# Channel-mix matrices loaded as f64 words and converted behind the attention stage, without a DRAM scratch; the copy of k by the scalar engine

## The chip, the cores and the metric

One NeuronCore of a Trainium2 chip runs the whole kernel. Its engines are TensorE (PE; its weight loads are listed apart as PEld), VectorE (DVE), ScalarE (ACT), GpSimd (POOL) and SyncE (SP), which here only issues DMAs. Each engine works through its own queue in order; a matmul, a copy or a DMA issue that waits for data holds up all that stands behind it in that queue. The metric is the time of one execution on the device, in microseconds (us).

## The reference

Three layers follow each other, on 4 batches of 768 tokens with 384 channels:

```
# 1. linear attention with decay, 8 heads of 48
y[t] = r[t] @ (state + (u*k[t]) v[t]^T);  state = w[t]*state + k[t] v[t]^T
# 2. four attention experts of 64 dims, causal softmax, the best two of four per token, weighted
q, k, v = x@wq[e], x@wk[e], x@wv[e];  out += mask*gate * (softmax(q k^T/8) @ v @ wo[e])
# 3. channel mix (all three matrices come as float64)
xk, xr = mu_k*x + (1-mu_k)*x_prev,  mu_r*x + (1-mu_r)*x_prev
out = sigmoid(xr @ w_r) * (max(xk @ w_k, 0)**2 @ w_v)      # 384x384, 384x1024, 1024x384
```

## The kernel before

The three layers are written as three streams: **A** (layer 1, two heads at a time: 16 pairs), **B** (layer 2, `phase_b`, one batch at a time) and **C** (layer 3; `c_thin` in units of 256 tokens for batches 0 to 2, `c_wide` in units of 384 tokens for batch 3). Products that must be exact are made of a high and a low part of each factor (`split`), three matmuls for one.

Stage 1 runs A for all batches, with about the first one and three quarters batches of B beside it. When A is done, its SBUF (pool `pA`) is given up, and stage 2 runs the rest of B beside C; then C's wide units end the kernel. `run_all` hands out pieces of the streams by their costs, and a list scheduler then fixes the order of instructions on each engine. Stage 2 lets C go first by a lead of a tenth of its cost (`CLAG`).

[...] `c_convert` turns them into two fp32r parts in 34 blocks of 256 or 192 columns during stage 1. Each block (`split_block`) is a load on SP's queue (L797), a scale on ACT (L802), three integer operations on DVE (L803 to L805), the high part on ACT (L807), the low part on POOL (L808), and two stores to a DRAM scratch on SP's queue (L817). At the start of stage 2, `c_weights` reads the scratch back with six loads from POOL's queue (L833). The names are `c_raw` for the words, `c_w` for the value, `c_hi` and `c_lo` for the parts, and ckh, ckl, crh, crl, cvh, cvl for the parts of the three matrices.

In C, `c_mix` makes the two mixed inputs (`mh`, `ml` by L858 to L865), `c_hidden` the product with w_k (`ph`, eight groups of nine matmuls, L871), its square on POOL (`rl`, L891) and its parts (`hh`, `hl`), and `c_out` the products with w_r (`pz`) and w_v (`pvo`).

In B, `proj` makes q and k of two experts. The high part of k must also stand on the other 64 partitions, and a DMA on SP's queue copies it there (L571, 32 of them). `trans` copies transposed probabilities (`at`) from PSUM, some on DVE (L692), the rest on ACT (L694): the tables `AT_DVE` (batches below `AT_B`) and `AT_DVE2` say which.

Of the kernel before, what the change touches and what calls it, by code (L numbers as in the profile page):

```python
# [112 lines left out]
def rwkv_moe_kernel(ctx, tc, r, k, v, w, u, wg, wq, wk, wv, wo, mu_k, mu_r, w_k, w_v, w_r, out):  # L113
# [666 lines left out]
    CW = (("ck", w_k, KT, FF), ("cr", w_r, KT, DM), ("cv", w_v, NF, DM))  # L780
    csc = {
        nm: [nc.dram_tensor(f"{nm}_{x}_scratch", (128, n0 * n1), F32R, kind="Internal").ap() for x in "hl"]
        for nm, _, n0, n1 in CW
    }

    CQ_L, CQ_S = nc.sync, nc.sync

    def split_block(src, hi, lo, n):
        T = lambda tag, dt: pA.tile([128, n], dt, tag=tag, name=tag, bufs=CB, padded_shape=[128, 256])
        if src.dtype != I64:  # L790
            st = T("c_w1", F32)
            nc.sync.dma_start(st, src)
            nc.scalar.copy(hi, st)
            nc.gpsimd.tensor_tensor(out=lo, in0=st, in1=hi.bitcast(F32), op=OP.subtract)
            return
        raw = pA.tile([128, 2 * n], U32, tag="c_raw", name="c_raw", bufs=CB, padded_shape=[128, 512])
        CQ_L.dma_start(raw, src.bitcast(U32))  # L797
        wd = raw.rearrange("p (n two) -> p two n", two=2)
        wlo, whi = wd[:, 0], wd[:, 1]
        w1 = T("c_w1", U32)  # L800
# [1 line left out]
        nc.scalar.activation(out=w1.bitcast(F32), in_=whi.bitcast(F32), func=AF.Copy, scale=2.0 ** -112)  # L802
        V.tensor_scalar(out=w1, in0=w1, scalar1=3, scalar2=None, op0=OP.logical_shift_left)  # L803
        V.scalar_tensor_tensor(out=w1, in0=whi, scalar=0x80000000, in1=w1, op0=OP.bitwise_and, op1=OP.bitwise_or)
        V.scalar_tensor_tensor(out=w1, in0=wlo, scalar=29, in1=w1, op0=OP.logical_shift_right, op1=OP.bitwise_or)  # L805
        w1f = w1.bitcast(F32)
        nc.scalar.copy(hi, w1f)  # L807
        (V if CONV_DVE else nc.gpsimd).tensor_tensor(out=lo, in0=w1f, in1=hi.bitcast(F32), op=OP.subtract)  # L808

    def c_convert():  # L810
        pend = []
        for nm, src, n0, n1 in CW:
            n = 256 if n1 % 256 == 0 else n1 // 2
            for j in range(n0):
                for o in range(0, n1, n):
                    for d, t in pend:
                        CQ_S.dma_start(d, t)  # L817
                    hi = pA.tile([128, n], F32R, tag="c_hi", name="c_hi", bufs=CB, padded_shape=[128, 256])
                    lo = pA.tile([128, n], F32R, tag="c_lo", name="c_lo", bufs=CB, padded_shape=[128, 256])
                    split_block(src[j * 128 : (j + 1) * 128, o : o + n], hi, lo, n)  # L820
                    at = j * n1 + o
                    pend = [(csc[nm][i][:, at : at + n].bitcast(F32), t.bitcast(F32)) for i, t in enumerate((hi, lo))]
                    yield 1
        for d, t in pend:
            CQ_S.dma_start(d, t)
# [399 lines left out]
```

## Time and profile before

| | us |
|---|---|
| three timed runs, median (lowest to highest) | 726.49 (726.14 to 726.61) |
| profiled execution | 727.12 |
| its span in the trace | 725.4 |
| PE, PEld busy | 672.8, 585.4 |
| DVE, ACT, POOL busy | 497.9, 409.2, 299.7 |

The span is what the trace covers; the 1.7 us that the profiled execution has beyond it lie around it. The shares of busy time are averages over stages that differ, so the tables below cut the span into stretches. Stage 1 reaches to about 326 us, where the six loads of the weights are issued; the matmuls of layer 3 begin at 333 us, and B ends at about 645 us. The granted clock of TensorE was 0.984 of full speed over the span.

### The profile page before, as it was taken

Reading aid. Unit: us, or ns where it says so; the run is one execution under the profiler, and the core shown is the slowest. Engines: PE = TensorE matmul, PEld = TensorE weight load, DVE = VectorE, ACT = ScalarE, POOL = GpSimd, SP = SyncE. Lnnn points to the kernel's source line nnn. Section 1 sums busy time; section 2 is a strip of 40 time slices with the busy share of each in tenths; the row PEclk is TensorE's granted clock in tenths of the full one; section 3 lists DMA queues with packets and bytes.
Section 4 is the critical chain, followed back from the end, with each engine's and each line's share of the span. In section 5 each row is a group of like instructions: output and inputs, shape, how many; then the busy total and the mean of one; then the engine's idle time right before and its main releaser. Section 6 shows DMA issues by size and latency. Waiting matters only on the chain.

```text
span 725.4 us, 13681 instructions
## 1 busy us (share of the span) xinstructions
PE 672.8 (93%) x4938; PEld 585.4 (81%) x4938; DVE 497.9 (69%) x938; ACT 409.2 (56%) x1117; POOL 299.7 (41%) x397
## 2 busy tenths in 40 slices
PE   5887978889799999997999999999999999999995
PEld 4776856676577786866999899889898888989995
DVE  8988899998999888754543756556457573729520
ACT  3554556666576566656735657465556656534530
POOL 5876444343445222204625435362343515352320
PEclk9999899999999999999999999999999999999999
DMA  8797666668677653159320103211101101220001
GB/s 157 152 184 173 176 180 175 170 174 251 148 198 186 170 126 83 33 187 411 100 67 11 45 12 99 98 34 44 55 34 44 23 13 34 86 68 23 12 23 38
DMA packets 144205, 77.88 MB, mean 107 GB/s; under 512 B 109824, under 2 KB 138752, under 8 KB 143616
## 3 DMA queue, kind: packets, MB, share of 16 engines
q1 hardware_dynamic: 139936, 64.73, 35.1%
q0 software_dynamic: 864, 7.47, 2.6%
q10 hardware_dynamic: 3328, 4.72, 1.8%
q8 instruction: 41, 0.67, 0.4%
q14 instruction: 36, 0.29, 0.1%
HBM read 47.40 MB, written 23.99 MB: 98 GB/s over the span
## 4 chain that ended last, share of the span: by engine, by line
PE 64%; DVE 18%; DMA 8%; issue 4%; ACT 3%; POOL 1%; SPq 1%; ACTq 0%; DVEq 0%; POOLq 0%
PE ph L871 14%; PE pvo L871 14%; PE pz L871 5%; PE pa L710 5%; PE pq L518 4%; PE pt L681 3%; PE po L518 3%; PE py L368 3%; PE pv L518 3%; DMA c_raw<-in_moe_w_v_dram 2%; DVE ex L246 2%; PE psc L624 2%; PE pg L329 2%; DVE suf L220 2%; DVE rt L255 2%
## 5 line engine op out<-in xcount | busy, mean ns | idle before, releaser
L633 DVE TENSOR_REDUCE st<-psc 128x1 f32<-128x384 f32 (+4 forms) x128 | 62.1, 499 | 56.4 <-PE psc L629 41.3
L891 POOL TENSOR_TENSOR rl<-rl 128x256 f32<-128x256 f32 (+1 forms) x88 | 59.3, 678 | 78.5 <-ACT rl L890 78.3
L865 POOL TENSOR_TENSOR ml<-m,mh 128x256 fp32r<-128x256 f32 x54 | 40.6, 751 | 108.5 <-ACT mh L864 97.4
L645 ACT ACTIVATE A<-psc,st 128x384 f32<-128x384 f32 (+4 forms) x128 | 68.8, 542 | 20.2 <-DVE st L642 13.3
L871 PE MATMUL ph<-mh,ckh 128*128 128x256 f32 (+1 forms) x264 | 78.8, 299 | 0.9 <-ACT m L858 0.8
L871 PE MATMUL ph<-mh,ckl 128*128 128x256 f32 (+1 forms) x264 | 76.9, 292 | 1.5 <-DMA ckl<-ck_l_scratch 1.5
L338 POOL TENSOR_SCALAR_AFFINE_SELECT at<-at 128x512 f32<-128x512 f32 x48 | 44.7, 932 | 79.2 <-ACT at L337 79.0
L871 PE MATMUL ph<-ml,ckh 128*128 128x256 f32 (+1 forms) x264 | 76.9, 294 | 0.0
L871 PE MATMUL pvo<-cvh,hh 128*128 128x384 f32 x192 | 65.5, 341 | 0.0
L329 PE MATMUL pg<-rt,kt 128*128 128x256 f32 x192 | 53.8, 407 | 12.3 <-DVE um L307 5.8
L894 POOL TENSOR_TENSOR hl<-rl,hh 128x256 fp32r<-128x256 f32 x72 | 53.8, 756 | 27.0 <-ACT hh L892 26.7
L871 PE MATMUL pvo<-cvl,hh 128*128 128x384 f32 x192 | 64.6, 336 | 0.0
L871 PE MATMUL pvo<-cvh,hl 128*128 128x384 f32 x192 | 64.0, 336 | 0.0
L681 PE MATMUL pt<-ident,A 128*128 128x128 f32 x336 | 57.7, 275 | 0.0
L624 PE MATMUL psc<-k,q 128*128 128x384 f32 (+4 forms) x128 | 49.0, 383 | 9.0 <-ACT A L645 6.2
L890 ACT ACTIVATE rl<-ph 128x256 f32<-128x256 f32 (+1 forms) x88 | 35.5, 405 | 37.6 <-PE ph L871 26.2
L871 PEld LDWEIGHTS ph<-mh,ckh 128*128 128x128 f32 x264 | 49.9, 189 | 3.3 <-ACT m L858 1.0
L710 PE MATMUL pa<-at,vs 128*64 128x384 f32 (+2 forms) x288 | 52.1, 425 | 0.5 <-ACT at L694 0.5
L871 PEld LDWEIGHTS ph<-mh,ckl 128*128 128x128 f32 x264 | 50.0, 190 | 1.8 <-DMA ckl<-ck_l_scratch 1.8
L871 PEld LDWEIGHTS ph<-ml,ckh 128*128 128x128 f32 x264 | 49.9, 190 | 1.5 <-issue 1.5
L329 PEld LDWEIGHTS pg<-rt,kt 128*128 128x128 f32 x192 | 34.4, 197 | 19.8 <-DVE um L307 6.8
L861 DVE SCALAR_TENSOR_TENSOR m<-x2c,mu,m 128x256 f32<-128x256 f32 (+1 forms) x66 | 35.2, 539 | 20.4 <-ACT m L858 15.8
(172 smaller groups left out, 1917.3 us busy)
## 6 DMA issues: line engine op xcount, KB each, us to landing
x_scratch<-xs SPq DMA_DIRECT2D x24, 288.0 KB, 4.0
x<-x_scratch SPq DMA_DIRECT2D x6, 1152.0 KB, 8.4
nw<-in_w_dram SPq DMA_DIRECT2D x32, 144.0 KB, 3.7
nk<-in_k_dram SPq DMA_DIRECT2D x32, 144.0 KB, 3.1
nr<-in_r_dram SPq DMA_DIRECT2D x32, 144.0 KB, 2.8
nv<-in_v_dram SPq DMA_DIRECT2D x16, 288.0 KB, 3.2
out_dram<-rg SPq DMA_DIRECT2D x24, 192.0 KB, 1.9
c_raw<-in_moe_w_k_dram SPq DMA_DIRECT2D x12, 256.0 KB, 3.3
```

The lines of the kernel that those rows point to most:

```text
L329: nc.tensor.matmul(pg[:, x * 2 * C : (x + 1) * 2 * C], lhsT=kt[:, c * C : (c + 1) * C], rhs=rt[:, c].rearrange("p h x -> p (h x)"), start= ...
L338: nc.gpsimd.affine_select(out=av, in_=av, pattern=[[0, 4], [1, C]], compare_op=OP.is_gt, fill=0.0, base=0, channel_multiplier=-1)
L518: nc.tensor.matmul(out, lhsT=a, rhs=c, start=i == 0, stop=i == n - 1)
L624: nc.tensor.matmul(o, lhsT=qs[e][:, tsl], rhs=ks[e][:, s0:s1], start=True, stop=False, skip_group_check=True)
L633: nc.vector.tensor_reduce(out=st[:, si : si + 1], in_=o, axis=AX.X, op=OP.max, negate=True)
L645: nc.scalar.activation(out=A[:, s0:s1], in_=p[:, 0 : s1 - s0], func=AF.Exp, bias=nm, accum_out=st[:, 3 + si : 4 + si])
L681: nc.tensor.transpose(pt[:, (j - j0) * 128 : (j - j0 + 1) * 128], A[:, j * 128 : (j + 1) * 128], ident)
L710: nc.tensor.matmul(pa[64 * e : 64 * e + 64, t0:HALF], lhsT=vs[:, j, 2 * pr + e], rhs=at[e][:, c0 : c0 + HALF - t0], start=j == 0, stop=j = ...
L865: eng.tensor_tensor(out=lo[:, j], in0=m1, in1=hi[:, j].bitcast(F32), op=OP.subtract)
L871: nc.tensor.matmul(out, lhsT=a, rhs=c, start=i == 0, stop=i == n - 1)
L891: nc.gpsimd.tensor_tensor(out=rl_, in0=rl_, in1=rl_, op=OP.mult)
L894: eng.tensor_tensor(out=hl[:, m], in0=rl_, in1=hh[:, m].bitcast(F32), op=OP.subtract)
```

## The change

The constants: the table of `at` copies on DVE is empty for batch 0, and batch 1 now takes the longer table that held for batches 2 and 3. The copy of k to the other partitions is made by ACT from PSUM in batches 1 to 3; batch 0 keeps the DMA.

The conversion and the scratch are gone from stage 1. Stage 2 begins with 17 loads of 64-bit words (512 or 384 elements in each of 128 partitions) on POOL's queue, into the room that the parts of the same piece will take; ahead of them the first input tile of C now also goes through POOL's queue. The conversion of a piece is the same seven steps without the two stores: the value is built in a tile that borrows the room of the second mixed input (`mh1`, `ml1`), and the parts overwrite the words. Three pieces are converted before the first product with w_k, the others between its eight groups (1, 1, 1, 2, 2, 2, 5), and the second mixed input of the first unit comes after them all.

```diff
-DUP = "dma"
-AT_DVE = ((5, 0), (4, 0))
+AT_DVE = ()
 AT_DVE2 = ((5, 0), (4, 0), (3, 0))
-AT_B = 2
+AT_B = 1
...
                         split(ks[e][own, sl], kls[e][own, sl], src)
-                        if DUP == "act":
+                        if b:
                             nc.scalar.copy(ks[e][oth, sl], src)
...
                         else:
                             nc.sync.dma_start(ks[e][oth, sl].bitcast(F32), ks[e][own, sl].bitcast(F32))
...
+    CW = tuple(
+        [("ck", w_k, j, 512 * g, (4, 2, 128)) for g in range(2) for j in range(KT)]
+        + [("cr", w_r, j, 0, (1, 2, DM)) for j in range(KT)]
+        + [("cv", w_v, j, 0, (1, 2, DM)) for j in range(NF)]
+    )
+    def c_weight_loads(pW):
+        raws = []
+        for nm, src, j, o, (m, x, n) in CW:
+            words = 2 if src.dtype == I64 else 1
+            t = pW.tile([128, words * m * n], U32, tag=f"{nm}{j}_{o}", name="cw", bufs=1, padded_shape=[128, 2 * m * n])
+            nc.gpsimd.dma_start(t, src[j * 128 : (j + 1) * 128, o : o + m * n].bitcast(U32))
+            raws.append(t)
+        return raws
+    def c_convert(pW, raws, pool, tags=("mh1", "ml1")):
...
+                nc.scalar.activation(out=w1f, in_=whi.bitcast(F32), func=AF.Copy, scale=2.0 ** -112)
+                V.tensor_scalar(out=w1, in0=w1, scalar1=3, scalar2=None, op0=OP.logical_shift_left)
+                V.scalar_tensor_tensor(out=w1, in0=whi, scalar=0x80000000, in1=w1, op0=OP.bitwise_and, op1=OP.bitwise_or)
+                V.scalar_tensor_tensor(out=w1, in0=wlo, scalar=29, in1=w1, op0=OP.logical_shift_right, op1=OP.bitwise_or)
+            t = pW.tile([128, m, x, n], F32R, tag=f"{nm}{j}_{o}", name="cp", bufs=1)
+            v = w1f.rearrange("p (m n) -> p m n", n=n)
+            nc.scalar.copy(t[:, :, 0], v)
+            nc.gpsimd.tensor_tensor(out=t[:, :, 1], in0=v, in1=t[:, :, 0].bitcast(F32), op=OP.subtract)
+            wsp[nm, j, o] = t
+            yield 0
...
+        mixes[0] = [c_load(pool, *units[0], n, 1, nc.gpsimd), {}]
+        conv = c_convert(pW, c_weight_loads(pW), pool)
+        for _ in mix(0, 0):
+            pass
+        for _ in next_n(conv, KT):
+            yield 0
...
+            if u == 0:
+                side = (list(next_n(conv, i)) for i in (1, 1, 1, 2, 2, 2, 5))
+                side = (c for g in (side, mix(u, 1)) for c in g)
+                yield from c_side(c_hidden(pool, pst, mixes[u][1][0], n, 1, hs), side, 1)
...
-    conv = stream(c_convert(), nconv * CV)
-    run_all(sB, sA, conv, until=sA)
-    for _ in conv[0]:
-        pass
+    run_all(sB, sA, until=sA)
...
-        c_weights(pW)
```

The order of instructions, row by row as each engine's queue has them (line of the kernel, operation, output and inputs, size of the output, repeats). DVE in stage 1, where batch 0 of B begins, before: `rt`, `xs`, `kt`, `suf` and `ex` belong to A, `c_w` to the conversion.

```order
L246 SCALAR_TENSOR_TENSOR ex<-wx,d1f 128x774
L255 TENSOR_TENSOR rt_86<-ptr,ex 48x3x128 x4
L383 TENSOR_TENSOR xs<-py,xs 128x384
L803 TENSOR_SCALAR c_w_842<-c_w_842 128x256
L804 SCALAR_TENSOR_TENSOR c_w_842<-c_raw,c_w_842 128x256
L383 TENSOR_TENSOR xs<-py,xs 128x384
L805 SCALAR_TENSOR_TENSOR c_w_842<-c_raw,c_w_842 128x256
L256 TENSOR_TENSOR ku<-ku,nr 128x576
L220 SCALAR_TENSOR_TENSOR suf<-wx,d_77 128x775
```

The same place in the changed kernel (its line numbers are lower by two here):

```order
L244 SCALAR_TENSOR_TENSOR ex<-wx,d1f 128x774
L253 TENSOR_TENSOR rt_86<-ptr,ex 48x3x128 x4
L381 TENSOR_TENSOR xs<-py,xs 128x384
L254 TENSOR_TENSOR ku<-ku,nr 128x576
L381 TENSOR_TENSOR xs<-py,xs 128x384
L257 TENSOR_REDUCE cc<-ku 128x12
L218 SCALAR_TENSOR_TENSOR suf<-wx,d_77 128x775
```

The three `c_w` rows are gone, here and 33 times more down to the end of stage 1.

POOL at the start of stage 2, before: six loads, then the low part of the mixed input.

```order
L338 AFFINE_SELECT at<-at 128x512 x5
L833 DMA ckh<-ck_h_scratch 128x3072
L833 DMA ckl<-ck_l_scratch 128x3072
L833 DMA crh<-cr_h_scratch 128x1152
L833 DMA crl<-cr_l_scratch 128x1152
L833 DMA cvh<-cv_h_scratch 128x3072
L833 DMA cvl<-cv_l_scratch 128x3072
L844 MEMSET x2c 128x3
L616 MEMSET st_4601 128x6
L865 TENSOR_TENSOR ml_3893<-m_3894,mh_3892 128x256
```

The same place after (`cw` are the words of a piece, `cvs` the value, `cp` its parts):

```order
L336 AFFINE_SELECT at<-at 128x512 x5
L826 MEMSET x2c 128x3
L827 DMA x2c<-x_scratch 128x3x256
L790 DMA cw<-in_moe_w_k_dram 128x1024 x6
L790 DMA cw<-in_moe_w_r_dram 128x768 x3
L790 DMA cw<-in_moe_w_v_dram 128x768 x8
L847 TENSOR_TENSOR ml_3473<-m_3474,mh_3472 128x256
L612 MEMSET st_4302 128x6
L815 TENSOR_TENSOR cp<-cvs,cp 128x4x128 x2
L847 TENSOR_TENSOR ml_3473<-m_3479,mh_3472 128x256
```

Eighteen DMA issues stand where six stood, and the low parts of the weights are made between those of the mixed input.

PE just ahead of the first product with w_r (`pz`), before:

```order
L518 MATMUL pq<-x,wkl 128x384
L518 MATMUL pq<-x,wkh 128x384
L723 MATMUL pb<-ident,y 128x128
L710 MATMUL pa<-at_5025,vs 64x384
L710 MATMUL pa<-at_4726,vs 64x384
L710 MATMUL pa<-at_5025,vs 64x384
L710 MATMUL pa<-at_4726,vs 64x384
L871 MATMUL pz<-crh,mh_3941 128x384
```

The same place after; `psc`, `pt` and `pa` are now of the next batch of B:

```order
L620 MATMUL psc<-k_4621,q_4619 128x384
L621 MATMUL psc<-kl_121,q_4619 128x384
L677 MATMUL pt<-ident,A 128x128 x2
L706 MATMUL pa<-at_5206,vs 64x384
L706 MATMUL pa<-at_5162,vs 64x256
L706 MATMUL pa<-at_5206,vs 64x256
L706 MATMUL pa<-at_5162,vs 64x128
L706 MATMUL pa<-at_5206,vs 64x128
L853 MATMUL pz<-cp,mh_3732 128x384 x2
```

From the first `ph` to the first `pz` there were 167 matmuls in PE's queue before, 72 of them `ph`; now there are 303, again 72 of them `ph`. The 136 more are B's.

## Rows read from the trace of the kernel before

**Rows 1.** The stretches: PE, PEld, DVE, ACT, POOL busy (instructions), clock, DMA share, GB/s.
```profile
20.00:80.00 60.00, 51.79 (x466) 40.95 (x462) 52.75 (x76) 30.77 (x76) 46.17 (x42) 0.91 0.77 169
80.00:250.00 170.00, 148.67 (x1235) 118.42 (x1231) 156.36 (x316) 108.36 (x301) 70.33 (x79) 0.98 0.70 182
250.00:326.00 76.00, 72.14 (x627) 58.23 (x625) 57.12 (x124) 45.42 (x127) 15.91 (x21) 1.00 0.44 113
326.00:376.00 50.00, 46.26 (x298) 40.65 (x299) 27.65 (x49) 31.11 (x84) 23.14 (x37) 1.00 0.54 198
376.00:641.00 265.00, 265.00 (x1803) 241.09 (x1802) 149.66 (x290) 155.66 (x450) 111.09 (x166) 1.00 0.15 46
```
**Rows 2.** The chain that ended last, shares of the span by engine.
```profile
PE 64%; DVE 18%; DMA 8%; issue 4%; ACT 3%; POOL 1%; SPq 1%; ACTq 0%; DVEq 0%; POOLq 0%
```
**Rows 3.** The conversion on DVE, 80 to 250 us: line, operation, count | busy us, mean ns.
```profile
L805 DVE SCALAR_TENSOR_TENSOR c_w<-c_raw,c_w 128x192 uint32<-128x192 uint32 x22 | 11.6, 536 | 0.2
L804 DVE SCALAR_TENSOR_TENSOR c_w<-c_raw,c_w 128x192 uint32<-128x192 uint32 x22 | 7.7, 362 | 0.2
L803 DVE TENSOR_SCALAR c_w<-c_w 128x192 uint32<-128x192 uint32 x22 | 6.5, 302 | 1.0 <-ACT c_w L802 0.9
L805 DVE SCALAR_TENSOR_TENSOR c_w<-c_raw,c_w 128x256 uint32<-128x256 uint32 x10 | 5.5, 550 | 0.2
L804 DVE SCALAR_TENSOR_TENSOR c_w<-c_raw,c_w 128x256 uint32<-128x256 uint32 x10 | 4.3, 434 | 0.1
L803 DVE TENSOR_SCALAR c_w<-c_w 128x256 uint32<-128x256 uint32 x10 | 3.2, 324 | 1.1 <-ACT c_w L802 1.1
```
**Rows 4.** The conversion and the `at` copies elsewhere, whole span and 80 to 250 us.
```profile
L808 POOL TENSOR_TENSOR c_lo<-c_w,c_hi 128x192 fp32r<-128x192 f32 (+1 forms) x34 | 28.1, 830 | 47.7 <-ACT c_hi L807 27.4 <-issue 10.7 <-DMA cr_l_scratch<-c_lo 3.0
L802 ACT ACTIVATE c_w<-c_raw 128x192 f32<-128x192 f32 (+1 forms) x34 | 13.7, 402 | 12.0 <-DMA c_raw<-in_moe_w_v_dram 6.9 <-DMA c_raw<-in_moe_w_k_dram 2.6 <-DMA c_raw<-in_moe_w_r_dram 1.9
L807 ACT CAST c_hi<-c_w 128x192 fp32r<-128x192 f32 (+1 forms) x34 | 12.5, 374 | 13.2 <-DVE c_w L805 13.1
...
L692 DVE COPY at<-pt 128x512 f32<-128x512 f32 x8 | 5.5, 683 | 0.1
```
**Rows 5.** One line of the conversion: duration ns min/median/max, first and last start.
```profile
L805 DVE SCALAR_TENSOR_TENSOR c_w<-c_raw,c_w x34: 335/410/1252, 68.0 to 246.6; 128x192 uint32<-128x192 uint32 x22, 128x256 uint32<-128x256 uint32 x12
```
**Rows 6.** Copy of k: the ACT operation on its source, and PE's waits for the DMA.
```profile
L142 ACT CAST k<-pq x32: 453/474/478, 96.0 to 577.4; 64x384 fp32r<-64x384 f32 x32
...
PE psc L624 <- DMA k<-k: 2.2, 2, 1.7
```
**Rows 7.** POOL's queue from 324 us: start, duration, operation [idle before, releaser].
```profile
325.50 0.73 POOL L833 DMA_DIRECT2D ckh<-ck_h_scratch  x1 [14.92 <-PE pt L681]
326.22 0.55 POOL L833 DMA_DIRECT2D ckl<-ck_l_scratch  x1
...
328.30 0.59 POOL L833 DMA_DIRECT2D cvl<-cv_l_scratch  x1
...
331.42 0.73 POOL L865 TENSOR_TENSOR ml<-m,mh 128x256 fp32r<-128x256 f32 x1 [2.38 <-ACT mh L864]
```
**Rows 8.** PE at the first product of layer 3.
```profile
332.84 0.48 PE L871 MATMUL ph<-mh,ckh 128*128 128x256 f32 x2 [0.84 <-ACT m L858]
...
336.50 0.38 PE L871 MATMUL ph<-mh,ckl 128*128 128x256 f32 x1 [1.48 <-DMA ckl<-ck_l_scratch]
```
**Rows 9.** The chain of waits in order of time: start, us, what.
```profile
167.79 9.46 DMA c_raw<-in_moe_w_v_dram
...
326.22 10.23 DMA ckl<-ck_l_scratch
...
359.65 1.78 PE pz L871 x9
```
**Rows 10.** DMA issues: KB each, us from issue to landing.
```profile
cvl<-cv_l_scratch POOLq DMA_DIRECT2D x1, 1536.0 KB, 19.8
```

More of the change, by code (lines that the diff above doesn't have):

```diff
@@ L778, in rwkv_moe_kernel @@
     NF = FF // 128
[L780 to L800, printed above, removed]
-        V = nc.vector
[L802 to L825, printed above, removed]
-        yield 1
@@ new lines, in c_weight_loads @@
+    def c_weight_loads(pW):
[7 more added lines that the diff above has]
+    def c_convert(pW, raws, pool, tags=("mh1", "ml1")):
+        room = [
+            pool.tile([128, KT, TN], F32R, tag=t, name="cvs", bufs=1).rearrange("p k n -> p (k n)").bitcast(U32) for t in tags
+        ]
+        V = nc.vector
+        for i, ((nm, src, j, o, (m, x, n)), raw) in enumerate(zip(CW, raws)):
+            w1 = room[i % 2][:, 0 : m * n]
+            w1f = w1.bitcast(F32)
+            if src.dtype != I64:
+                nc.scalar.copy(w1f, raw.bitcast(F32))
+            else:
+                wd = raw.rearrange("p (n two) -> p two n", two=2)
+                wlo, whi = wd[:, 0], wd[:, 1]
+                nc.scalar.activation(out=w1f, in_=whi.bitcast(F32), func=AF.Copy, scale=2.0 ** -112)
[8 more added lines that the diff above has]
+            yield 0
@@ L875, in c_hidden @@
     def c_hidden(pool, pst, mix, n, bufs, res):
-        ckh, ckl = wsp["ck"]
+        ck = lambda j, m, x: wsp["ck", j, 512 * (m // 4)][:, m % 4, x]
         kh, kl = mix
@@ L885, in c_hidden @@
                 ph[:, 0:n],
-                [t for j in range(KT) for t in ((ckh[:, j, ms], kh[:, j]), (ckl[:, j, ms], kh[:, j]), (ckh[:, j, ms], kl[:, j]))],
+                [t for j in range(KT) for t in ((ck(j, m, 0), kh[:, j]), (ck(j, m, 1), kh[:, j]), (ck(j, m, 0), kl[:, j]))],
             ):
@@ L906, in c_out @@
                 pz[:, 0:DM],
-                [t for j in range(KT) for t in ((rh[:, j, cs], crh[:, j]), (rh[:, j, cs], crl[:, j]), (rl[:, j, cs], crh[:, j]))],
+                [t for j in range(KT) for t in ((rh[:, j, cs], cr(j, 0)), (rh[:, j, cs], cr(j, 1)), (rl[:, j, cs], cr(j, 0)))],
             ):
@@ L918, in c_out @@
             pv = pst("o", "pvo")
-            terms = [t for m in range(NF) for t in ((hh[:, m, cs], cvh[:, m]), (hh[:, m, cs], cvl[:, m]), (hl[:, m, cs], cvh[:, m]))]
+            terms = [t for m in range(NF) for t in ((hh[:, m, cs], cv(m, 0)), (hh[:, m, cs], cv(m, 1)), (hl[:, m, cs], cv(m, 0)))]
             for k in mm_seq(pv[:, 0:DM], terms, 8):
@@ L934, in rwkv_moe_kernel, with c_thin @@
     bdone = {"n": 0}
-    def c_thin(pool, pst, units, n):
+    def c_thin(pW, pool, pst, units, n):
         mixes, hs = {}, []
@@ L1076, in rwkv_moe_kernel @@
         thin_units = units_of(range(B - 1), TN)
-        thin = c_thin(pC, psum_of(psC, {x: ("c", 2) for x in "hzo"}), thin_units, TN)
+        thin = c_thin(pW, pC, psum_of(psC, {x: ("c", 2) for x in "hzo"}), thin_units, TN)
         left = B - sB[2]
@@ L1188, in rwkv_moe_kernel @@
         with ExitStack() as sg:
-            c_weights(sg.enter_context(tc.tile_pool(name="pW2", bufs=1, side="right")))
+            pW = sg.enter_context(tc.tile_pool(name="pW2", bufs=1, side="right"))
             pD = sg.enter_context(tc.tile_pool(name="pD2", bufs=1, side="left"))
+            for _ in c_convert(pW, c_weight_loads(pW), pD, ("cvs0", "cvs1")):
+                pass
             psD = sg.enter_context(tc.tile_pool(name="psD2", bufs=1, space=PSUM))
```

29 lines of the change are left out of this document (8 added, 21 removed).

## The prediction

> **What bounds the kernel now.** I read the stretches first [rows 1], then the chain of waits [rows 2, 9], then the groups by line for what the change takes out [rows 3, 4], and last the queues of POOL and PE where stage 2 begins [rows 7, 8].
>
> The stretches show two kernels. Up to 326 us DVE is the fullest engine: it is busy 156.36 of the 170 us from 80 to 250, or 92%, with ACT at 64%, POOL at 41% and PE at 87%. From 376 to 641 us PE is busy in all of the 265 us, its weight loads in 241.09, and DVE falls to 56% [rows 1]. The chain says the same: PE has 64% of it and DVE 18% [rows 2]; with PE leading in stage 2, DVE's part must come mostly from stage 1. So work taken off DVE is worth something before 326 us, and work given to DVE after 376 us is nearly free; what remains is the seam between them, where the change puts all of it at once.
>
> How tight is PE in stage 1? Its busy time leaves 170 - 148.67 = 21.3 us of idle from 80 to 250, which would cap any gain there. But the weight loads fill only 118.42 of 170 us, 70%, against 241.09 of 265, 91%, in the stretch where PE is certainly the bound [rows 1]. The Trainium skill (Perfetto Trace Analysis, Identifying the Most-Contended Engine) says that matmul busy time is no measure of PE's headroom, since pipelined matmuls overlap, and that weight-load busy time is; by it PE could do this stretch in 118.42 / 0.91 = 130 us and the gain could reach 40 us, where the busy time allows 21. The rows side with it so far as the two shares disagree there and not in stage 2.
>
> **The change, part by part.**
>
> *The conversion leaves stage 1.* On DVE 32 of the 34 blocks lie between 80 and 250 us: 11.6 + 7.7 + 6.5 + 5.5 + 4.3 + 3.2 = 38.8 us [rows 3]. The eight `at` copies of batch 0 go to ACT, 5.5 us more [rows 4]; ACT loses 26.2 us of conversion there and has room. DVE is left with 156.36 - 38.8 - 5.5 = 112.1 us. The gain has these bounds:
> - DVE alone, at the same 92%: 112.1 / 0.92 = 122 us, gain 48.
> - PE by busy time: if it cannot be fuller than the 95% it has from 250 to 326, 148.67 / 0.95 = 156.5 us, gain 13.5.
> - The pace of the stretch that has no conversion. From 250 to 326 us A and B run as they will run everywhere. DVE is there at 57.12 / 76 = 75%, and 112.1 / 0.75 = 149 us, gain 21; by matmuls, 627 in 76 us is 8.25 per us, 1235 at that pace take 150 us, gain 20.
>
> The third is the nearest row. I add a little, because ACT's queue also loses its waits for `c_raw` (6.9 + 2.6 + 1.9 = 11.4 us of idle [rows 4]; one of those loads stands in the chain for 9.46 us [rows 9]) and SP's queue loses 34 loads and 68 stores that stand between A's loads. I take 25 us, with 13 and 48 as the ends. Batch 1's four more `at` copies on DVE, 2.7 us, fall where DVE is at 75% and cost nothing; at 92% they would cost their 2.7.
>
> *Copy of k.* 24 of the 32 DMAs become 24 ACT copies of the 0.474 us that the like operation on the same source takes, 11.4 us in all [rows 6]. ACT is at 59% in stage 2 [rows 1], which hides them; uncovered they are the 11.4. PE waited 2.2 us in all for the DMA [rows 6]. I count a gain of 1, between -2 and 2; the PSUM bank is held up to two copies longer, with three banks in turn.
>
> *The seam.* Call S the issue of the first weight load, 325.50 now [rows 7]. Before, the first full product with w_k could go at S + 11 (336.50, after a wait for ckl [rows 8]) and the first `pz` came at S + 34.2 (359.65 [rows 9]). After, three things stand in that place.
> - Loads. POOL issues 18 DMAs and not 6. At 0.55 to 0.73 us each [rows 7] that is some 10 us before its first low part of the mixed input, which stood at S + 6. The same 7.47 MB move; the last landing took 19.8 us [rows 10] and hides behind the conversion.
> - The conversion on DVE. Pieces are now 512 or 384 columns. The three operations take 1.308 us for 256 columns and 1.200 for 192 [rows 3]: 0.108 per 64 columns. Carried on, 512 take 1.74 and 384 take 1.52: 6 x 1.74 + 11 x 1.52 = 27 us. The ends are 20 (a double piece costs as one) and 42 (as two).
> - B drawn forward. In PE's new order 303 matmuls stand between the first `ph` and the first `pz`, and not 167. The 167 took 359.65 - 332.84 = 26.8 us, 0.16 each, so the 136 more are 22 us of PE work taken from later: not a loss, as long as PE does them at its pace.
>
> The dense work up to `pz` is thus 34 + 22 = 56 us. DVE's own share beside such work is 27.65 / 50 = 55% [rows 1], so 31 us, and with the conversion 31 + 27 = 58, at 92% 63 us. The second mixed input of unit 0 comes after the last piece, about 3 us more (three columns of ACT, DVE, ACT, POOL, overlapping). 63 + 3 - 56 = 10 us lost. With a conversion of 20 us it is 2, with 42 it is 26.
>
> *After the seam* PE's work is what it was, C merely later against B by the 22 us. C's last units stand alone a little longer; the wide units of batch 3 can begin beside them, since B ends earlier. I take nothing for it.
>
> **Sum** against the profiled execution: 727.1 - 25 - 1 + 10 = 711.1 us; it stands 0.6 above the median of the timed runs, so 710.5, and I say 711.
>
> **The rivals.**
> 1. *DVE was the whole bound of stage 1.* Gain 48, loss 10: 727.1 - 48 - 1 + 10 - 0.6 = 687.5. For it: DVE at 92%, and the weight loads' 70%. Against it: from 250 to 326, without a conversion, DVE stays at 75% and the pace rises by little.
> 2. *PE takes over at once.* Gain 13.5, loss 10: 722.5 - 0.6 = 722. For it: PE busy 87% and 95%. Against: the weight loads.
> 3. *Slower: PE's queue stops at the seam.* Mechanism: conversion operations on DVE collide with POOL's low parts and loads, each takes longer than carried on, and since PE's queue is in order, the first `pz` with unconverted pieces stops B too. L805 took between 335 and 1252 ns, median 410, mean about 540 in the long run [rows 3, 5], so something stretches it already. At the upper end, 42 us, the loss is 26; with the pieces at twice my 27 us, 54, it is (31 + 54) / 0.92 + 3 - 56 = 39, and 727.1 - 25 - 1 + 39 - 0.6 = 739.5. It decides from a loss of 26 us on, where the gain of 25 + 1 is used up. Against it: 303 matmuls stand ahead of that place, and from 326 to 376 DVE has 22 us idle [rows 1]. The Trainium skill (SBUF — State Buffer, SBUF: two separate sides) states a rule that makes this worse: DVE and GpSimd share a pair of ports under an exclusive lock, and loads issued from POOL's queue can starve for descriptors while DVE holds it. No row shows that for these loads: before, they were issued at 0.55 us each while DVE had few such operations.
>
> **Chances.** My forecast (700 to 719) 0.50; rival 1 (below 700) 0.19; rival 2 (719 to 725) 0.16; no change to be told (725.0 to 728.0) 0.04; rival 3, slower, 0.11. Within 0.2%, 1.5 us, a measurement of this kernel can't tell from no change. Faster is 0.50 + 0.19 + 0.16 = 0.85, same 0.04, slower 0.11. The range for 8 in 10 goes from rival 1's 688 to the edge of no change, 727, with a tenth on each side; the likeliest case's own range is 700 to 719.
>
> **What would show it.** Right: no `c_w` on DVE before the seam, the pairs of A closer together, S at about 300 us and not 325.5, DVE at about 75% from 80 to there. At the seam DVE above 90% for some 60 us, the first `pz` about 66 us after S, and the conversion on DVE near 27 us. PE busy without a gap from there to B's end. Wrong: S not before 312 us (rival 2), S before 285 (rival 1), or idle PE of more than 20 us between S and the first `pz` with waits for `cp` or for the high parts (rival 3).

## The result, and the profile after

| | before | after |
|---|---|---|
| timed runs beside each other, median (lowest to highest), us | 726.46 (726.14 to 726.61) | 731.5 (730.3 to 732.58) |
| profiled execution, its span | 727.12, 725.4 | 731.66, 729.9 |
| DVE, ACT busy | 497.9, 409.2 | 500.1, 422.0 |

The change is slower by a factor of 1.007 (95% interval 1.0052 to 1.0087), by little but clear of the noise. 711 was forecast, with 0.11 for slower.

The stretches of the changed kernel, in the columns of [rows 1]; the cuts are the first load of stage 2 (294), the first `pz` (374) and B's end (612):

```profile
20.00:80.00 60.00, 52.89 (x497) 43.03 (x494) 51.91 (x77) 31.55 (x77) 43.77 (x40) 0.97 0.72 150
80.00:250.00 170.00, 163.95 (x1439) 136.18 (x1438) 138.94 (x262) 108.98 (x292) 47.49 (x56) 1.00 0.52 119
250.00:294.00 44.00, 43.13 (x386) 34.85 (x385) 32.20 (x66) 28.82 (x78) 8.62 (x12) 1.00 0.38 109
294.00:374.00 80.00, 59.67 (x339) 46.89 (x336) 63.02 (x125) 50.60 (x131) 46.89 (x57) 0.85 0.31 114
374.00:612.00 238.00, 234.47 (x1549) 211.09 (x1549) 139.55 (x254) 144.03 (x411) 95.05 (x143) 0.99 0.12 40
612.00:680.00 68.00, 65.70 (x410) 62.95 (x410) 46.55 (x68) 39.95 (x93) 41.80 (x52) 1.00 0.15 47
```

Stage 1 gained what it should and more: from 20 us to 294 PE has done 497 + 1439 + 386 = 2322 matmuls, and before it took until 326 for 466 + 1235 + 627 = 2328 [rows 1], so the gain is some 31 us. Then come 80 us with PE busy 59.67 of them, at a granted clock of 0.85; 298 matmuls had taken 50 us there [rows 1]. To place the loss I counted every matmul in both traces with its duration where PE is full (0.119 us for `ph` of 256 columns, 0.173 for `pz`, and so on): at equal work the changed kernel is 30 us ahead where A ends, 19 ahead at 323 us, 6 at 376, level at 400, 1 behind at 619 and 6 behind at the end. So 36 us are given back: 11 at once, 13 up to the first `pz`, 6 just behind it, 1 in the long run, 5 behind B's end. The later figures "by equal work" are the same count; they hold to about 1 us.

The chain that ended last, by engine, answers to [rows 2]: DVE's share has risen.

```profile
PE 62%; DVE 21%; ACT 6%; DMA 5%; issue 4%; POOL 1%; SPq 1%; POOLq 0%; DVEq 0%; ACTq 0%
```

The conversion on DVE, its rows alone, 285 to 400 us (line, operation, count | busy us, mean ns), against [rows 3]: 34.8 us in all.

```profile
L810 DVE SCALAR_TENSOR_TENSOR cvs<-cw,cvs 128x384 uint32<-128x384 uint32 x11 | 8.2, 741 | 0.2
L811 DVE SCALAR_TENSOR_TENSOR cvs<-cw,cvs 128x384 uint32<-128x384 uint32 x11 | 8.0, 730 | 0.2
L809 DVE TENSOR_SCALAR cvs<-cvs 128x384 uint32<-128x384 uint32 x11 | 5.6, 507 | 2.1 <-ACT cvs L808 2.0
L811 DVE SCALAR_TENSOR_TENSOR cvs<-cw,cvs 128x512 uint32<-128x512 uint32 x6 | 5.1, 846 | 0.1
L810 DVE SCALAR_TENSOR_TENSOR cvs<-cw,cvs 128x512 uint32<-128x512 uint32 x6 | 4.7, 786 | 0.1
L809 DVE TENSOR_SCALAR cvs<-cvs 128x512 uint32<-128x512 uint32 x6 | 3.2, 531 | 0.9 <-ACT cvs L808 0.9
```

POOL's queue at the seam (start, duration, operation [idle before, releaser]), against [rows 7]:

```profile
293.74 0.93 POOL L827 DMA_DIRECT2D x2c<-x_scratch  x1 [0.42 <-issue]
...
302.03 0.54 POOL L790 DMA_DIRECT2D cw<-in_moe_w_v_dram  x1 [1.89 <-DMA cw<-in_moe_w_k_dram]
...
310.71 0.54 POOL L790 DMA_DIRECT2D cw<-in_moe_w_v_dram  x1 [0.43 <-DMA cw<-in_moe_w_r_dram]
311.26 0.73 POOL L847 TENSOR_TENSOR ml<-m,mh 128x256 fp32r<-128x256 f32 x1
```

Each issue takes 0.54 to 0.57 us, as foreseen, but from the ninth weight load on each also waits until an earlier one has landed. The wait stands in the program, where each DMA of this queue waits for the one eight before it. POOL is held for 17.5 us, where 10 had been reckoned, and the first low part of the mixed input comes at S + 16.6 (S, the first weight load, is at 294.66). ACT's and PE's queues there, against [rows 8, 9]:

```profile
298.10 0.51 ACT L840 ACTIVATE m<-x2c,om 128x256 f32<-128x256 f32 x1 [4.14 <-DMA x2c<-x_scratch]
```

```profile
301.22 0.69 PE L620 MATMUL psc<-k,q 128*128 128x384 f32 x1 [5.66 <-ACT A L641]
303.01 0.80 PE L853 MATMUL ph<-mh,cp 128*128 128x256 f32 x2 [0.23 <-ACT cp L814]
304.81 0.79 PE L620 MATMUL psc<-k,q 128*128 128x512 f32 x1 [0.99 <-ACT A L641]
307.75 0.79 PE L620 MATMUL psc<-k,q 128*128 128x512 f32 x1 [1.59 <-ACT A L641]
...
322.59 0.44 PE L620 MATMUL psc<-k,q 128*128 128x384 f32 x1 [1.07 <-ACT x L739]
...
373.79 0.61 PE L853 MATMUL pz<-cp,mh 128*128 128x384 f32 x2
```

ACT stands for x2c with B's exps behind it, PE runs dry for 5.66 us, and then works through B's chain alone, one `psc` in 2.95 us, each waiting for the exp of the one before. The first `pz` is at S + 79, and S + 66 had been foreseen.

What PE waited for from S to the first `pz`, in its 20.3 us of idle time (us in total, times, longest):

```profile
PE psc L620 <- ACT A L641: 10.5, 5, 5.7
PE po L516 <- DVE y L722: 2.6, 2, 1.5
PE po L516 <- DVE avl L141: 1.8, 2, 1.6
...
PE ph L853 <- ACT cp L814: 0.2, 1, 0.2
```

PE hardly waits for the converted parts (`cp`). It waits for B's own work on ACT and DVE, which stands in those queues among the conversion's.

### The profile page after: what moved, and what is told of

It is laid out like the page before. It is cut to its first block, busy times and chain, and to the rows that moved or that the text cites. A ratio compares the mean times of both kernels' runs of the same rounds, so it can differ in the third digit from the quotient of the medians.

```text
span 729.9 us, 13301 instructions
## 1 busy us (share of the span) xinstructions
PE 676.2 (93%) x4938; PEld 588.7 (81%) x4938; DVE 500.1 (69%) x883; ACT 422.0 (58%) x1115; POOL 299.4 (41%) x392
## 4 chain that ended last, share of the span: by engine, by line
PE 62%; DVE 21%; ACT 6%; DMA 5%; issue 4%; POOL 1%; SPq 1%; POOLq 0%; DVEq 0%; ACTq 0%
PE pvo L853 12%; PE ph L853 10%; PE pa L706 5%; PE pq L516 5%; PE pz L853 4%; PE py L366 4%; PE pt L677 3%; PE pv L516 3%; PE po L516 3%; PE pg L327 3%; PE psc L620 3%; PE ptr L199 2%; PE psc L621 2%; DVE suf L218 2%; DVE st L629 2%
## 5 line engine op out<-in xcount | busy, mean ns | idle before, releaser
L853 PE MATMUL ph<-mh,cp 128*128 128x256 f32 (+1 forms) x528 | 108.1, 299 | 0.9 <-ACT rl L871 0.5
L853 PE MATMUL pvo<-cp,hh 128*128 128x384 f32 x384 | 100.9, 341 | 2.5 <-DVE rg L903 2.5
L872 POOL TENSOR_TENSOR rl<-rl 128x256 f32<-128x256 f32 (+1 forms) x88 | 62.4, 715 | 76.5 <-ACT rl L871 75.9
L853 PEld LDWEIGHTS ph<-mh,cp 128*128 128x128 f32 x528 | 85.2, 190 | 5.9 <-ACT rl L871 1.6
L853 PE MATMUL ph<-ml,cp 128*128 128x256 f32 (+1 forms) x264 | 76.0, 292 | 0.0
L853 PEld LDWEIGHTS pvo<-cp,hh 128*128 128x128 f32 x384 | 69.9, 190 | 4.5 <-DVE rg L903 3.5
L853 PE MATMUL pvo<-cp,hl 128*128 128x384 f32 x192 | 65.2, 340 | 0.0
L846 ACT CAST mh<-m 128x256 fp32r<-128x256 f32 (+1 forms) x66 | 28.1, 428 | 40.3 <-DVE m L843 29.5
L871 ACT ACTIVATE rl<-ph 128x256 f32<-128x256 f32 (+1 forms) x88 | 34.8, 405 | 26.1 <-PE ph L853 23.3
L853 PEld LDWEIGHTS ph<-ml,cp 128*128 128x128 f32 x264 | 49.7, 190 | 0.2 <-issue 0.2
L897 DVE RECIPROCAL rg<-rg 128x384 f32<-128x384 f32 x18 | 45.9, 2549 | 0.4
L873 ACT CAST hh<-rl 128x256 fp32r<-128x256 f32 (+1 forms) x88 | 37.1, 426 | 15.0 <-POOL rl L872 14.5
```

Of the source, the lines that this page charges most:

```text
L853: nc.tensor.matmul(out, lhsT=a, rhs=c, start=i == 0, stop=i == n - 1)
L872: nc.gpsimd.tensor_tensor(out=rl_, in0=rl_, in1=rl_, op=OP.mult)
L897: nc.vector.reciprocal(out=rg, in_=rg)
```

## The experiments

Each median stands beside runs of the kernel before made at the same time, whose median was 726.2 to 727.4 us; the ratio to it is given with its 95% interval. Two to three us between runs made at different times are not told apart.

### Where stage 1's gain comes from

**The small parts alone**, on the kernel before.

```diff
-AT_DVE = ((5, 0), (4, 0))
-AT_B = 2
+AT_DVE = ()
+AT_B = 1
-                        if DUP == "act":
+                        if b:
                             nc.scalar.copy(ks[e][oth, sl], src)
```

> The kernel before with the small parts of the change alone: the copy of k by ACT for batches 1 to 3, and the two tables of at copies. The prediction's terms: the k copy 1 us, and of the 25 us of stage 1 the share of the eight at copies of batch 0 (5.5 of 44.3 us of DVE), 3 us; together 720 to 724 against 726.2. Rival: the DMA and the copies were hidden, 725.5 to 727. Slower, over 728, would say that ACT's 11.4 us of copies stand in PE's way in stage 2.

728.16 us, 1.0021 (1.0002 to 1.0039): no gain, perhaps 1.5 us lost. In 80 to 250 us it does 30 matmuls fewer than before [rows 1], in the profiled execution, which at 730.61 us is the longest of this kernel's runs:

```profile
80.00:250.00 170.00, 147.03 (x1205) 116.58 (x1204) 150.72 (x306) 111.88 (x306) 65.02 (x76) 0.97 0.68 177
```

**Before, without DVE's three operations** (L803 to L805 left out).

> The kernel before without the three integer operations per block on DVE (some 40 us in stage 1); its loads, ACT's scale and high part, POOL's low part and the stores stay, so the weights' values are not the reference's. Theory D (DVE alone bounds stage 1 there): A ends 22 to 28 us earlier, and with no conversion in the seam nearly all of it is kept: 698 to 706 us. Theory L (the 34 loads and 68 stores on SP's queue and ACT's waits for the words hold A as well): A ends 8 to 15 us earlier, 711 to 719.

710.02 us, 0.9762 (0.9735 to 0.979): 16.7 less than the kernel before, 1 us below theory L's range. The same stretch, and POOL's first load of stage 2:

```profile
80.00:250.00 170.00, 156.26 (x1345) 128.63 (x1344) 132.36 (x250) 113.40 (x320) 68.70 (x81) 1.00 0.73 190
```

```profile
311.73 0.73 POOL L830 DMA_DIRECT2D ckh<-ck_h_scratch  x1 [14.03 <-DMA x_scratch<-xs]
```

110 matmuls more than before, where the change has 204 more; the first load is 13.8 us earlier and not 30.8. This profiled execution took 715.14 us, 5 more than the median, and by equal work it is 16 us ahead at 300 us and 11 at 326, so in the other runs the first load may well come earlier. Theory L is the nearer one: DVE's time is about half of the gain of 31 us, by the times and by equal work at 300. The rest goes with what stayed here (loads, stores, ACT's waits for the words); which of these was not taken apart.

### What the seam loses: the conversion

**No conversion** (as many loads and as large; the loaded fp32 numbers are the parts).

```diff
-            nc.gpsimd.dma_start(t, src[j * 128 : (j + 1) * 128, o : o + m * n].bitcast(U32))
+            nc.gpsimd.dma_start(t..., bass.AP(tensor=k.tensor, offset=0, ap=[[2048, 128], [1, 2 * m * n]]).bitcast(F32R))
...
+            wsp[nm, j, o] = raw
```

> The changed kernel with its 17 loads on POOL's queue as they are, but with no conversion at all: the loads bring fp32 numbers of k, which are used as parts, so the outputs are not the reference's. The changed kernel took 731.5 us, the one before 726.5; stage 1 ended 31 us earlier and about 31 us were lost again up to 400 us. Theory W (the conversion's work on DVE, ACT and POOL, and the waits for its parts, cost the seam): the loss falls to a few us, 700 to 708 us. Theory Q (the queues: 17 loads ahead of POOL's low parts, ACT waiting behind the first x2c): they are still there, so at most 8 us come back, 723 to 730. Theory T (C runs later against B, and its end stands alone): here the first pz stands 205 matmuls after the end of A and not 335, which gives 5 us at the end; by it alone 726.

711.36 us, 0.9796 (0.9752 to 0.9841): 20 us come back, 3 us short of theory W's range and far from Q's and T's. Some 15 of stage 1's gain stay lost (727.1 - 31 would be 696). By equal work this run is 30 us ahead at 290 us, 18 at 323, 15 at 340 and 15 still at 700: with the loads alone 15 us are lost, all of them up to 340 us, and none behind that or at the end.

**Without DVE's three operations** (L809 to L811 left out).

> The changed kernel without the three integer operations per piece on DVE (34.8 us in its trace); ACT's scale and high part, POOL's low part and all loads remain, so the weights' values are not the reference's. Theory W-DVE (DVE's part of the conversion is what the seam waits for): nearly all comes back, 702 to 710 us, DVE below 75% between 300 and 400 us, and no dip of the clock after 320. Theory W-chain (the chain ACT, DVE, ACT, POOL of 17 pieces with two rooms, the engines' queues and not DVE's time): half comes back, 715 to 722. Theory Q (POOL's queue): 725 to 731, the first low part still 17 us after the first load.

718.17 us, 0.988 (0.9837 to 0.9924): 13 back. W-chain's range holds it; W-DVE does not.

**Without POOL's low part.**

```diff
-            nc.scalar.copy(t[:, :, 0], v)
-            nc.gpsimd.tensor_tensor(out=t[:, :, 1], in0=v, in1=t[:, :, 0].bitcast(F32), op=OP.subtract)
+            nc.scalar.copy(t, v[:, :, None, :].to_broadcast([128, m, 2, n]))
```

> The changed kernel (731.5 us) without POOL's 17 low parts: ACT's copy of the high part writes both places, so the weights' low parts are not the reference's. Theory P (rival 3 of the prediction: DVE's operations and POOL's collide, and POOL, behind its 17 loads, finishes the pieces): the 17 pieces' three operations on DVE fall from 34.8 us to 28 or 30, the first pz comes before S + 65 and not at S + 80, 720 to 726 us. Theory D (DVE's own time in the seam): they stay above 33 us, and the time within 3 us of the changed kernel, 728 to 732.

716.94 us, 0.9857 (0.9829 to 0.9885): 14.6 back, below theory P's range, and the first `pz` at 348.64, S + 55, with all of DVE's operations still there. They are shorter beside a free POOL, 30.3 us in all; of the 384-column ones:

```profile
L811 DVE SCALAR_TENSOR_TENSOR cvs<-cw,cvs 128x384 uint32<-128x384 uint32 x11 | 7.4, 673 | 0.3
L810 DVE SCALAR_TENSOR_TENSOR cvs<-cw,cvs 128x384 uint32<-128x384 uint32 x11 | 6.7, 606 | 0.2
L809 DVE TENSOR_SCALAR cvs<-cvs 128x384 uint32<-128x384 uint32 x11 | 4.6, 421 | 1.0 <-ACT cvs L808 1.0
```

The collision is there, but it is 4.5 us of DVE, not 14.6 us of time. The Trainium skill (SBUF — State Buffer, SBUF: two separate sides) says that a DVE operation with two inputs in SBUF and a GpSimd operation that reads SBUF lock each other out of a shared port pair. L810 and L811, which have two, took 741 and 730 ns and take 606 and 673 here: they agree. L809 has one such input and fell too, from 507 to 421, so the rows don't show that the second input is what matters.

Taking out either engine's part gives back 13 or 15 of the 20 us that the whole conversion is worth, so these are not two separate costs that add up. A piece goes ACT, DVE, ACT, POOL, and only two pieces are in the rooms `mh1` and `ml1` at a time: in the changed kernel two pieces wait for POOL, which is held until 311 us, and hold both rooms. Without POOL's part the conversion goes on during the loads: DVE is busy 23.30 of the 29 us from 294 to 323, and 17.14 in the changed kernel. A shorter chain and an earlier start are thus not told apart here.

**Four rooms** for the 384-column pieces, every operation kept.

```diff
             w1 = room[i % 2][:, 0 : m * n]
+            if n == DM:
+                w1 = room[i % 2][:, i // 2 % 2 * DM : (i // 2 % 2 + 1) * DM]
```

> The changed kernel (731.5 us) with four rooms for the values of the 11 pieces of w_r and w_v and not two: each borrowed tile holds two values of 384 words. Every operation stays. Theory R (the chain's length): the 11 last pieces follow each other in some 2.5 us and not 3.15, the first pz comes 7 us earlier, and 5 to 9 us come back: 722 to 727. Theory S (the engines' work): the pieces wait elsewhere, 729 to 733.

728.21 us, 1.0019 (1.0 to 1.0038): 3.3 less than the changed kernel, the first `pz` 8.1 us earlier:

```profile
365.68 0.59 PE L855 MATMUL pz<-cp,mh 128*128 128x384 f32 x2
```

The chain is shorter as theory R has it (the 11 last low parts on POOL follow each other in 2.3 us and not 3.15), but 3.3 us are less than it asked for. The order changed too: 263 matmuls stand between the first `ph` and the first `pz` and not 303, at 0.237 us each. On the better version of below the rooms gave nothing:

> The best version so far (721.1 us: loads on SP's queue, x2c in its own pool, the wide units' first product by ACT) with the same four rooms. Theory R: the first pz comes before 355 us and not at 362, 3 to 7 us less, 714 to 718. Theory S: 720 to 723.

723.9 us, 0.9957 (0.9942 to 0.9971), against 0.9928 without them: 1 us above theory S's range. **w_v in pairs**, four long turns for eight short ones, on the same version:

> The best version so far (721.1 us) with two rooms, and w_v in four pieces of 2 x 384 words and not eight of 384: four turns of the chain less, each of the four longer. Theory R: a turn's fixed part goes, the first pz some 5 us earlier, 716 to 719. Theory S: the DVE work falls only by the fixed part of 12 operations, 2 to 3 us, and the time by 1: 719.5 to 721.5.

717.12 us, 0.9852 (0.9824 to 0.9881): the time that R gave, but not its sign. The first `pz` comes at 359.9 us and not 362.2, 2.3 us earlier where R has 5, and by equal work both traces are 10 us ahead at 400. So the length of the chain may be part of the 15 us that the conversion costs in the seam (20, less 5 at the end); how much, the runs do not settle, since with every edit the scheduler also puts another number of B's matmuls ahead of `pz`.

**w_k converted in stage 1**, by the old way through the scratch, w_r and w_v in the seam.

> w_k is converted in stage 1 in 12 blocks and goes through a DRAM scratch as before; w_r and w_v, 11 pieces, are converted in stage 2 as in the change. DVE gets 12 x 1.31 = 16 us back in stage 1 and has 11 x 1.98 = 22 us and not 34.8 in the seam. Theory W (the conversion's work in the seam): the loss falls faster than the gain, since the first products with w_k need no conversion: gain of stage 1 about 18 us of the 31, loss 10 to 12, so 716 to 722 us. Theory Q (POOL's queue): 13 loads in place of 17, loss 20, 727 to 731. Theory G (a gain of stage 1 is given back whatever is done, since PE's order is bound later): 725 to 727.

732.29 us, 1.0076 (1.0056 to 1.0096): all three theories missed. By equal work it is 19 us ahead where A ends, and has lost that by 380 us: less is gained, and the seam costs nearly as much with 11 pieces as with 17.

### What the seam loses: the loads

**Loads and first x2c on SP's queue** (`nc.gpsimd.dma_start` to `nc.sync.dma_start` for the 18).

> The changed kernel with the 17 loads and the first x2c on SP's queue and not POOL's. Theory Q (POOL's low parts stand behind 17 issues, ACT's first mix behind an x2c that is itself issued by POOL): the first low part comes 5 to 10 us after the loads begin and not 17.5, PE's clock does not fall to 0.59 in the 20 us after, and 8 to 15 us come back: 716 to 723. Theory W (the conversion's work): the low parts come earlier, but the first pz stays where DVE lets it, and the time stays within 3 us of the changed kernel: 728 to 732. SP's own loads for B may stand behind the 17: then slower, 733 to 738.

725.6 us, 0.9985 (0.9964 to 1.0006): 6 us back, between the two theories. The first low part comes at 299.18 us and not 311.26. The loads themselves land no sooner (KB each, median us from issue to landing; POOL's queue in the changed kernel, then SP's), and ACT's first mix, which waits for x2c, comes only 0.5 us earlier (297.63 us). So what came back goes with POOL being free:

```profile
cw<-in_moe_w_k_dram POOLq DMA_DIRECT2D x6, 512.0 KB, 7.7
```

```profile
cw<-in_moe_w_k_dram SPq DMA_DIRECT2D x6, 512.0 KB, 8.0
```

**x2c in its own pool besides.**

```diff
+    pX = ctx.enter_context(tc.tile_pool(name="pX", bufs=1))
-            mixes[u] = [c_load(pool, *units[u], n, 1), {}]
+            mixes[u] = [c_load(pX, *units[u], n, 1), {}]
```

> As the run with all loads on SP's queue (725.6 us), and the input tile x2c of the thin units lies in a pool of its own, so that its first load goes out during stage 1. Theory X (ACT stood 3 to 4 us at the head of its queue for x2c, B's exps behind it, PE ran dry for 6 us, and its clock fell): ACT's wait goes, PE has no gap over 2 us before the first ph, the granted clock stays above 0.9 from 300 to 320, and 5 to 9 us come back: 717 to 721. Rival: ACT stands in the same place for the first words of w_k, which land 7 us after their issue, and PE's gap stays: 724 to 727.

723.28 us, 0.9956 (0.9925 to 0.9987). ACT's first mix now comes at 293.21 us, as the loads begin, and PE's gap stayed, now for the first converted pieces (5.69 us): the rival named the right wait, and the time is between the two. **w_k in twelve pieces of 256**, three of them between two groups of `ph`, on the version with the tail edit (below) shortens it. PE's first `ph` there without and with the small pieces:

> The same best version with w_k in twelve pieces of 256 words and not six of 512: the first three land after half the bytes, and there are 23 conversions. Theory C (PE's gap of 5.7 us at the first ph is the landing and conversion of the first pieces): the gap falls to 2 to 3 us and the granted clock stays up, 717 to 720. Rival (the six more pieces cost DVE 3 to 4 us more, and the gap is that of other waits): 721 to 724.

```profile
302.24 0.80 PE L854 MATMUL ph<-mh,cp 128*128 128x256 f32 x2 [5.56 <-ACT cp L815]
```

```profile
299.60 0.50 PE L854 MATMUL ph<-mh,cp 128*128 128x256 f32 x2 [1.64 <-ACT cp L815]
```

721.09 us, 0.9905 (0.9878 to 0.9932), and 721.13 without: the gap fell as theory C said, and the time did not; the first `pz` came at 373.6 us and not 362.2, with 325 matmuls ahead of it and not 294. With the four rooms as well the first `pz` is at 358.2:

> The best version so far with w_k in twelve pieces of 256 words (alone it closed PE's gap at the first ph and gave nothing back, 721.1) and the four rooms. Theory R: the six more pieces lengthened the chain by what the earlier start had given; with the rooms the earlier start is kept: 711 to 716. Theory S: 719 to 722.

716.63 us, 0.9853 (0.9824 to 0.9883), 0.6 outside R's range. With the pairs of w_v in their place:

> The best version of the second call (721.1 us: loads on SP's queue, x2c in its own pool, the wide units' first product by ACT) with w_k in twelve pieces of 256 words and w_v in four of 2 x 384. If what the earlier start gives (PE's gap of 5.6 us at the first ph) is kept because the chain of pieces is shorter: 712 to 716. If the gains don't add, since what is won early is waited for again at the first pz: 717 to 720.

722.03 us, 0.9924 (0.9906 to 0.9941): the gains don't add, and it is slower still than that case allowed.

**No loads and no conversion** (one small tile stands for all weights).

> As the run without any conversion (711.4 us), and without the 17 loads: all parts of the weights are one small tile of fp32 numbers that is loaded at the kernel's start, so the outputs are not the reference's. Only the first x2c is loaded in the seam. Theory L (the loads: they land 7 to 11 us late, the first products wait for them, and PE has only B's chain meanwhile): PE's gap at the seam goes, the granted clock stays above 0.9, 8 to 13 us come back, 698 to 703. Theory B (B's chain alone is too thin for PE when A has ended, loads or not, until unit 0's input is mixed): PE busy below 16 of 20 us from 300 to 320 as before, 707 to 711.

701.01 us, 0.965 (0.9634 to 0.9667): theory L. By equal work this run is 27 us ahead at 290 us and 26 at 680: it loses nothing in the seam. (Its stage 1 gained 27 us and not 30; why stays open.) The stretch from 300 to 320 us in the changed kernel, without conversion, and without loads too:

```profile
300.00:320.00 20.00, 12.97 (x51) 9.57 (x52) 12.17 (x23) 11.16 (x28) 8.85 (x15) 0.59 0.88 335
```

```profile
300.00:320.00 20.00, 13.89 (x62) 10.65 (x60) 6.99 (x12) 8.46 (x23) 7.20 (x13) 0.63 1.03 304
```

```profile
300.00:320.00 20.00, 17.19 (x111) 14.93 (x112) 10.36 (x21) 14.44 (x43) 10.41 (x15) 0.91 0.17 53
```

In the middle one no engine is half busy but PE, whose clock is down. What is full there are the 16 DMA engines (share 1.03), as in the changed kernel. Its PE queue and then POOL's show what PE waits for:

```profile
303.31 0.79 PE L620 MATMUL psc<-k,q 128*128 128x512 f32 x1 [1.12 <-ACT A L641]
306.25 0.79 PE L620 MATMUL psc<-k,q 128*128 128x512 f32 x1 [1.59 <-ACT A L641]
309.20 0.90 PE L719 MATMUL pb<-ident,y 128*128 128x128 f32 x3 [1.59 <-ACT A L641]
```

```profile
311.31 0.53 POOL L789 DMA_DIRECT2D cw<-in_k_dram  x1 [1.07 <-DMA cw<-in_k_dram]
311.85 0.74 POOL L828 TENSOR_TENSOR ml<-m,mh 128x256 fp32r<-128x256 f32 x1
```

The same chain of B alone, and C's first low part behind the last load.

| | first ph, first pz (us) | matmuls between, in PE's queue | us for each |
|---|---|---|---|
| before [rows 8, 9] | 332.84, 359.65 | 167 | 0.161 |
| no loads, no conversion | 302.56, 323.7 | 134 | 0.158 |
| no conversion | 299.01, 342.56 | 178 | 0.245 |
| no POOL part | 303.19, 348.64 | 197 | 0.231 |
| no DVE part | 300.91, 350.95 | 211 | 0.237 |
| loads on SP | 305.00, 364.75 | 292 | 0.205 |
| after | 303.01, 373.79 | 303 | 0.234 |

These are averages over two stretches. Up to about 320 us the loads set the pace, also with no conversion at all: 51, 62 and 111 matmuls from 300 to 320 (above). The same three runs from there to the first `pz` of the changed kernel, and that kernel's first half of it:

```profile
323.00:374.00 51.00, 43.21 (x265) 34.87 (x264) 45.88 (x95) 36.63 (x99) 29.85 (x32) 0.93 0.05 17
```

```profile
323.00:374.00 51.00, 50.16 (x330) 46.74 (x331) 23.15 (x40) 31.39 (x84) 25.86 (x39) 0.94 0.12 39
```

```profile
323.00:374.00 51.00, 50.96 (x333) 48.93 (x334) 27.46 (x42) 28.05 (x73) 21.60 (x31) 1.00 0.10 32
```

```profile
323.00:350.00 27.00, 23.99 (x156) 19.84 (x155) 25.55 (x42) 21.73 (x56) 20.01 (x22) 1.00 0.03 9
```

Here the loads are over (DMA share 0.05) and make no difference: 330 and 333 matmuls. With the conversion there are 265, and DVE is busy 45.88 of 51 us, 90%, and 25.55 of 27 up to 350.

### The end, and DVE's other work

**First product of the wide units' inputs by ACT**, on the version with loads on SP and x2c in its own pool.

```diff
-            if (M1_ACT >> i) & 1 and bufs == 1:
+            if (M1_ACT >> i) & 1:
```

> As the run before it (loads on SP's queue, x2c in its own pool), and the first product of the mixed inputs of the two wide units is made by ACT and not by DVE, 12 operations, 7.8 us in the trace of the changed kernel. Theory E (the 5 us lost after 600 us are DVE's: the wide mixes fall on the reciprocals of the thin units, DVE 99% busy from 620 to 640): 3 to 5 us less than the run before it. Rival (C stands alone for longer, and waits on its own chain of ph, rl, hh): within 1 us of it.

721.13 us, 0.9928 (0.9903 to 0.9952): 2 less, in the direction of theory E and within the noise. DVE from 620 to 640 us without and with the edit (third value):

```profile
620.00:640.00 20.00, 18.83 (x107) 17.06 (x106) 19.78 (x27) 12.74 (x31) 13.48 (x16) 1.00 0.01 2
```

```profile
620.00:640.00 20.00, 19.19 (x112) 18.55 (x111) 17.75 (x23) 16.28 (x35) 13.52 (x15) 1.00 0.01 2
```

On the kernel before:

> The kernel before (726.5 us) with the one edit of the wide units (first product of the mixed inputs by ACT). Theory E (the 5 us at the end came with the change, since C runs later against B and the wide mixes fall on the thin units): here nothing is to be had, 726 to 727.5. Rival (the end is bound by DVE in either order): 722 to 725.

727.15 us, 1.0 (0.9978 to 1.0023): nothing to be had there, so DVE does not bind that end before the change. **All at copies on ACT** (`AT_DVE2 = ()`) on the version with the tail edit:

> The best version so far (loads on SP's queue, x2c in its own pool, the wide units' first product by ACT, 721.1 us) with all at copies on ACT: DVE loses 18 copies of 0.68 us from 400 us on, 12 between 300 and 400 (8.1 us) and 6 before. Theory D (DVE's time is what the seam lacks; 34.8 us of conversion cost about 14 there, 0.4 us per us): 3 to 5 us less, 716 to 718. Rival (ACT's in-order queue, on which the chain of exps runs, pays for it as for the copies of the run with the small parts alone): 721 to 724.

723.54 us, 0.9932 (0.9903 to 0.9961): the rival. 8 us less work on DVE in the seam gave nothing; ACT, which took it, may have paid for it.

The fastest versions that keep the whole computation are at 716.6 and 717.1 us.

## Why the prediction was wrong

1. *Stage 1, 25 us with ends 13 and 48*: right, and a little small (31). The bound by PE's busy time was passed: by equal work the stretch from 80 to 250 us gained 25 us, where PE's idle time had allowed 21.3. The Trainium skill (Perfetto Trace Analysis, Identifying the Most-Contended Engine) had said that matmul busy time is no measure of headroom. The rows agree, but by little: the granted clock rose from 0.98 to 1.00 [rows 1], and 148.67 us of busy time at full clock, some 146, would have allowed 24. The reason given was off: DVE's operations are about half of the gain, and the `at` copies, together with the copy of k, gave nothing.
2. *Copy of k, 1 us, and batch 1's `at` copies at nothing*: not seen; alone they cost 0 to 3 us with batch 0's.
3. *The seam, 10 us with ends 2 and 26*: this step failed. Some 30 us were lost there by 400 us, by equal work, and two terms of its sum were wrong. First, the loads were in the sum at nothing: the last landing "hides behind the conversion", and POOL's 10 us entered no term. They cost 15 us: the run without conversion loses that much up to 340 us, and the run without loads too loses nothing. Second, DVE was to be at 92% from S on, and the 136 matmuls of B drawn forward were "not a loss, as long as PE does them at its pace", 0.16 us each. DVE was busy 17.14 of 29 us up to 323, 59%, with both rooms held behind POOL's loads, and at 90% only after that; and PE's matmuls took 0.234 each: 303 of them 70.8 us and not 49. The 0.16 was read where B and C run side by side [rows 8, 9]; here B waited for its own work on ACT and DVE. The run without loads and conversion has 0.158 for 134 matmuls, so such a pace is there when both streams have their data.
4. *Loads, 10 us of POOL's queue*: 17.5, since the issues wait for landings. *Conversion, 27 us of DVE (20 to 42)*: 34.8, inside. Its price was taken as DVE occupancy, 58 us at 92%. DVE was busy 62.4 us from S to the first `pz`, which at 92% would be 68 us and not 79: most of the 13 us by which `pz` came late are DVE's idle time in the first stretch. The mean over the seam, 79%, hides that one part was starved and the other nearly full.
5. *The end, nothing*: 5 us. DVE is busy 19.89 of 20 us from 620 to 640 in the changed kernel; on the edit there see above.
6. *Rival 3* named the place, PE's in-order queue at the seam. Half of its mark came true: 20.3 us of idle PE between S and the first `pz`, where it asked for over 20. The other half did not: the waits were not for `cp` (0.2 us) but for B's own work. Its mechanism, the collision with POOL, is 4.5 us of DVE; and loads starved on POOL's queue do not show, since they land there as soon as on SP's (7.7 and 8.0 us).

So of the 36 us given back, the loads are 15 by equal work, and the conversion the rest. By the times the conversion is 20 (5 of them, by equal work, at the end) and the loads 10, the run without loads having gained less in stage 1; SP's queue gives back 6 of them. What splits the conversion's 15 in the seam between DVE's time, the chain's length and the order ahead of `pz` stays open: taking out DVE's operations gave back 13, but it shortens the chain and changes the order too.
